# Linear attention and MLP on one core: full-width matmuls for the ninth chunk, another schedule for batches 0 and 1

## The chip, the cores and the metric

The kernel runs on one core of one Trainium2 chip. The metric is device time in microseconds (us). Before the change it is 336.48 us, the median of three runs (336.4 to 340.16). The profile is one execution; its span is about 2 us shorter than the timed runs, so spans are compared with spans and times with times. Every run compared here is in the fast state; one timed run of one experiment was slow (322.38 us in e7, where the other three took 316.51 to 321.17), and it is left out of the ratio.

TensorE is called PE, its weight loads PEld, VectorE DVE, ScalarE ACT, and SP the engine whose queue issues most transfers. Names of tiles in the code and the profiles: `eq` is exp(q), `eqT` its transpose, `ek` and `ekr` are exp(k) of the 512 rows and of the remainder, `vm` and `vr` the cast v of the two, `pkv` the PSUM tile of kv, `po` that of the attention's output, `xn` and `xnT` the normalised x and its transpose, `ptr` the PSUM tile of a transpose on PE.

## The reference, cut to what matters

```python
# q, k, v: 8 batches, 8 heads, 576 rows, 64 columns
q_s = softmax(q, over the 64 columns)
k_s = softmax(k, over the 576 rows)
kv  = einsum('bhsd,bhse->bhde', k_s, v)        # 64 x 64 for each head
x   = einsum('bhsd,bhde->bhse', q_s, kv)       # heads side by side: 576 x 512
xn  = (x - mean) / sqrt(var + 1e-6) * g_ln     # over the 512
out = x + relu(xn @ w_ch1) @ w_ch2             # 512 -> 2048 -> 512
```

A batch has 576 rows: 512 of them make one chunk of four blocks of 128 rows, and 64 remain. The kernel gathers the eight remainders into a ninth chunk, two batches to a block of 128 rows.

## The kernel before

Chunk c's MLP is a list of PE steps, and the work that prepares later chunks is hung between them at step numbers. Each engine is given its instructions in this order; in the traces below ACT (8.93 us) and DVE (2.96 us) stand still at one that waits for a transfer, with work that is ready behind it. `mm1` is the first layer (`ph`, then relu into `hT`), `mm2` the second (`pc`, then `ot`). In chunk 0 there are 128 steps of `mm1` with 256 columns and 64 steps of `mm2`; in the others 64 and 64, all of 512 columns (only the last block of chunk 8's `mm2` is cut into 32 of 256).

```python
    def po_mm(c, t, i):
        if i == 0:
            pobox["p"] = att_ps.tile([P, DM], FP32, tag="a", name="po")   # 2 PSUM buffers
        po = pobox["p"]
        j = i % NP
        if c < B:
            nc.tensor.matmul(po[:, j*P : j*P+P], eqTs[c][:, t, j, :], kv_sb[:, c, j, :],
                             start=True, stop=True)
        else:                        # ninth chunk: one batch = 64 of the 128 rows
            ps = slice(64 * (i // NP), 64 * (i // NP) + 64)
            nc.tensor.matmul(po[ps, j*P : j*P+P], eqTs[c][:, t, j, ps],
                             kv_sb[:, 2*t + i // NP, j, :], start=True, stop=True)

    def x_out(c, t):                 # divide by the softmax sum, then the statistics
        x = xs[c][0]
        nc.vector.tensor_mul(x[:, t]..., pobox["p"]..., eqs[c][2][:, t].to_broadcast([P, H, D]))
        stats(c, t, x[:, t])         # bn_stats, bn_aggr, xn: all on DVE

    def prep_side(b, a0, a1):        # exp_q, one DMA transpose of exp(q), exp_k, casts, sums
        ...
    def load_batch(b):               # allocate; three DVE memsets; k, v, q, then the remainders
        ...
    # first_batch() ...
        for i in (2, 0, 1):          # q, k, v of batch 1 wait for a part of w1
            nc.gpsimd.tensor_copy(out=raws[1][i][0:1, 0, 0, 0:1], in_=w1_sb[0:1, 0, 1024:1025])
            load_main(nc.sync, 1, i, 0, H)
        load_kvrem(nc.sync, 1)
        nc.gpsimd.tensor_copy(out=gate, in_=raws[1][2][:, 0, 0, 0:4])
        for g4 in range(4):
            load_w2(g4)
        ...
        for t in range(T):
            sum_q(0, t)
            nc.vector.tensor_mul(eq[:, t], eq[:, t], rq[:, t].to_broadcast([P, H, D]))
            eq_pT(0, t, nc.vector)   # PE transpose, copied out of PSUM by DVE
    # ... [cut]
        run(mlp_steps(0), [(90, lambda: load_batch(2))]
            + prep_side(1, 20, 70) + attn_side(1, 56, 76, 78, 108, True))
        for c in range(1, B):
            if c == 1:
                side += prep_side(2, 4, 50); side += attn_side(2, 40, 60, 64, 96)
            elif c + 1 < B:
                side += attn_side(c + 1, 2, 22, 26, 58)
            else:
                side += attn_side(C9, 0, 0, 20, 60)
            if c + 2 < B:
                side += [(1, lambda b=c + 2: load_batch(b))]
                side += prep_side(c + 2, 90 if c == 1 else 66, 126)
```

The softmax here doesn't subtract the row's maximum and nothing guards it: scores larger than these inputs give would overflow.

## Time and profile before

Stages are cut at the first `mm1` matmul of each chunk, read from the timeline or the chain of waits (which differ by up to 0.2 us).

| stage | us | PE busy | granted clock |
|---|---|---|---|
| first attention, to 29.7 | 29.7 | 8.93 | 0.90 |
| chunk 0 (with batch 1's attention) | 51.5 | 38.94 | 0.83 |
| chunk 1 | 35.2 | 31.01 | 0.95 |
| chunks 2 to 6, each | 29.8 | 29.70 | 1.00 |
| chunk 7 (with the ninth chunk's attention) | 36.6 | 36.49 | 1.00 |
| chunk 8 and the tail | 31.9 | 27.59 | 1.00 |

A full chunk costs 29.8 us, so the excess lies in the beginning and in chunk 7. The view of busy time by stretch of the kernel before says the same; its columns are stretch, length, busy us (and count) of each engine, granted PE clock, share of the DMA engines (it can read above 1: 1.03 in a stretch further down) and GB/s:

```profile
29.70:81.20 51.50, 38.94 (x246) 25.18 (x247) 22.77 (x49) 13.16 (x26) 4.30 (x7) 0.83 0.78 162
81.20:116.40 35.20, 31.01 (x164) 14.77 (x164) 21.77 (x51) 17.57 (x34) 2.20 (x4) 0.95 0.75 182
116.40:146.20 29.80, 29.70 (x163) 14.47 (x164) 22.05 (x51) 13.54 (x25) 2.98 (x5) 1.00 0.80 195
265.40:302.00 36.60, 36.49 (x160) 15.14 (x160) 13.48 (x22) 8.86 (x16) 2.16 (x4) 1.00 0.15 44
```

The waits of PE in the kernel before, longest first (engine, line and tile that waited, what it waited for: us in total, times, longest):

```profile
PE ptr L452 <- DVE eq L512: 15.3, 4, 9.0
PE ptr L452 <- DVE xn L268: 7.4, 7, 2.2
PE po L253 <- DMA eqT<-eq: 7.1, 2, 3.5
PE pkv L221 <- ACT ek L133: 4.2, 1, 4.2
PE pkv L221 <- DVE vr L148: 1.1, 1, 1.1
```

PE waited twice, 3.5 us each, for a DMA transpose of exp(q): once in chunk 0 and once in chunk 1 (15.86 and 7.65 us of transpose in the chain of waits). In chunk 7 PE is never idle, and still it takes 6.8 us too long. Where the time goes shows in the weight loads of the timeline there (start, length, engine, line, operation, shape; in brackets the idle time before it):

```profile
270.36 0.11 PEld L259 LDWEIGHTS <-eqT 128*64 128x64 bf16 x1 [0.42 <-issue]
270.53 0.10 PEld L306 LDWEIGHTS <-w_sb 128*128 128x128 bf16 x1
270.85 0.11 PEld L259 LDWEIGHTS <-eqT 128*64 128x64 bf16 x1 [0.23 <-issue]
271.03 0.10 PEld L306 LDWEIGHTS <-w_sb 128*128 128x128 bf16 x1
271.35 0.11 PEld L259 LDWEIGHTS <-eqT 128*64 128x64 bf16 x1 [0.23 <-issue]
```

A load of 64 columns sits behind an idle gap of 0.23 or 0.42 us, and from one half matmul to the next, with one 512-column matmul between them, 0.49 us pass. The 512-column matmul alone needs 0.216 (8.63 us for 40 of them in the chain of waits), so the half one costs 0.28 us. Why a half-width load has this gap no run here shows; e1 below shows that the cost goes with the half width: chunk 7 falls from 36.6 to 31.7 us.

### The profile page before, as it was taken

Reading aid. Unit: us, or ns where it says so; the run is one execution under the profiler, and the core shown is the slowest. Engines: PE = TensorE matmul, PEld = TensorE weight load, DVE = VectorE, ACT = ScalarE, POOL = GpSimd, SP = SyncE. Lnnn points to the kernel's source line nnn. Section 1 sums busy time; section 2 is a strip of 40 time slices with the busy share of each in tenths; the row PEclk is TensorE's granted clock in tenths of the full one; section 3 lists DMA queues with packets and bytes.
Section 4 is the critical chain, followed back from the end, with each engine's and each line's share of the span. In section 5 each row is a group of like instructions: output and inputs, shape, how many; then the busy total and the mean of one; then the engine's idle time right before and its main releaser. Section 6 shows DMA issues by size and latency. Waiting matters only on the chain.

```text
span 333.9 us, 4180 instructions
## 1 busy us (share of the span) xinstructions
PE 291.4 (87%) x1603; PEld 148.3 (44%) x1620; DVE 180.5 (54%) x389; ACT 123.7 (37%) x227; POOL 32.4 (10%) x62
## 2 busy tenths in 40 slices
PE   0257575799959999999999999999999999999994
PEld 0154454444424454455445544544554433444443
DVE  4754267705426959745962874597279215520112
ACT  4315432301962055625804551581353043205500
POOL 4403000002000110110010011002000100010021
PEclk9995969699998999999999999999999999999999
DMA  9999994922990859939996962958106201111023
GB/s 204 204 192 329 229 143 59 347 50 92 299 207 2 188 168 309 175 82 359 177 207 204 266 135 80 331 128 159 63 2 119 101 33 31 31 63 65 0 47 79
DMA packets 76643, 49.74 MB, mean 149 GB/s; under 512 B 45392, under 2 KB 74320, under 8 KB 76624
## 3 DMA queue, kind: packets, MB, share of 16 engines
q1 hardware_dynamic: 67872, 35.26, 44.6%
q0 software_dynamic: 8752, 14.22, 17.8%
q8 instruction: 12, 0.20, 0.3%
q14 instruction: 7, 0.06, 0.1%
HBM read 36.96 MB, written 9.44 MB: 139 GB/s over the span
## 4 chain that ended last, share of the span: by engine, by line
PE 73%; DMA 15%; DVE 7%; SPq 1%; issue 1%; POOL 1%
PE ph L306 33%; PE pc L353 29%; DMA eqT<-eq 7%; PE pc L364 4%; DMA w_sb<-in_moe_w_ch_dram 3%; DMA ktr<-in_k_dram 3%; DMA kt<-in_k_dram 2%; PE pkv L221 2%; DVE st L266 2%; PE po L259 2%; PE po L253 2%; DVE x L276 2%; SPq L105 1%; DVE xn L268 1%; PE pc L375 1%
## 5 line engine op out<-in xcount | busy, mean ns | idle before, releaser
L306 PE MATMUL ph<-xnT,w_sb 128*128 128x512 bf16 x512 | 128.6, 380 | 0.4 <-DVE rq L178 0.4
L294 ACT ACTIVATE hT<-ph 128x512 bf16<-128x512 f32 x112 | 66.9, 597 | 134.8 <-PE ph L306 134.8
L353 PE MATMUL pc<-w_sb,hT 128*128 128x512 bf16 x481 | 110.0, 382 | 1.0 <-issue 0.2
L353 PEld LDWEIGHTS <-hT 128*128 128x128 bf16 x496 | 47.7, 98 | 58.0 <-DVE hT L292 2.3
L306 PEld LDWEIGHTS <-w_sb 128*128 128x128 bf16 x512 | 45.6, 98 | 48.2 <-DMA xnT<-xn 0.9
L335 DVE SCALAR_TENSOR_TENSOR ot<-pc,rstd,x 128x512 f32<-128x512 f32 (+1 forms) x37 | 27.1, 732 | 52.1 <-PE pc L353 36.3
L341 POOL DMA_DIRECT2D out_dram<-ot x32 | 18.1, 565 | 251.9 <-DVE ot L335 240.3
L253 PE MATMUL po<-kv_sb,eqT 128*128 128x128 bf16 x128 | 26.8, 227 | 7.7 <-DMA eqT<-eq 7.1
L276 DVE TENSOR_TENSOR x<-po,rq 128x512 bf16<-128x512 f32 x32 | 22.0, 687 | 19.0 <-PE po L259 13.0
L221 PE MATMUL pkv<-vm,ek 128*128 128x129 bf16 x112 | 25.5, 229 | 4.2 <-ACT ek L133 4.2
L177 DVE TENSOR_REDUCE zq<-eq 128x8 f32<-128x512 bf16 x36 | 23.7, 659 | 5.5 <-ACT eq L165 5.5
L268 DVE SCALAR_TENSOR_TENSOR xn<-x,mv,g_bc 128x512 bf16<-128x512 bf16 x32 | 24.1, 752 | 1.1
L292 DVE TENSOR_SCALAR hT<-ph 128x512 bf16<-128x512 f32 x16 | 11.0, 688 | 22.4 <-PE ph L306 22.4
L320 PE MATMUL ph<-xnT,w_sb 128*128 128x256 bf16 x128 | 22.9, 328 | 0.0
L266 DVE BATCH_NORM_STATS2 st<-x 128x6 f32<-128x512 bf16 x32 | 22.2, 694 | 1.1
L253 PEld LDWEIGHTS <-eqT 128*128 128x128 bf16 x128 | 12.6, 102 | 20.5 <-DMA eqT<-eq 7.8
L165 ACT ACTIVATE eq<-qt 128x512 bf16<-128x512 f32 x32 | 18.0, 621 | 6.4 <-DMA qt<-in_q_dram 6.0
L133 ACT ACTIVATE ek<-kt 128x512 bf16<-128x512 f32 x32 | 18.2, 620 | 1.9 <-DMA kt<-in_k_dram 1.7
L320 PEld LDWEIGHTS <-w_sb 128*128 128x128 bf16 x128 | 14.3, 118 | 4.8 <-issue 1.3
L221 PEld LDWEIGHTS <-ek 128*128 128x128 bf16 x128 | 13.4, 108 | 5.5 <-ACT ek L133 4.5
L452 PE MATMUL ptr<-ident,eq 128*128 128x128 bf16 x16 | 2.4, 306 | 15.3 <-DVE eq L512 15.3
L364 PE MATMUL pc<-w_sb,hT 128*128 128x512 bf16 x62 | 14.7, 393 | 0.3 <-issue 0.2
(66 smaller groups left out, 147.7 us busy)
## 6 DMA issues: line engine op xcount, KB each, us to landing
out_dram<-ot POOLq DMA_DIRECT2D x32, 256.0 KB, 3.2
qt<-in_q_dram SPq DMA_DIRECT2D x7, 1024.0 KB, 12.9
kt<-in_k_dram SPq DMA_DIRECT2D x7, 1024.0 KB, 7.4
vt<-in_v_dram SPq DMA_DIRECT2D x7, 1024.0 KB, 9.6
w_sb<-in_moe_w_ch_dram POOLq DMA_DIRECT2D x8, 512.0 KB, 11.3
qt<-in_q_dram SPq DMA_DIRECT2D x2, 512.0 KB, 4.3
ktr<-in_k_dram SPq DMA_DIRECT2D x8, 128.0 KB, 11.3
kt<-in_k_dram SPq DMA_DIRECT2D x4, 256.0 KB, 8.2
```

The lines of the kernel that those rows point to most:

```text
L177: nc.vector.reduce_sum(zq[:, t], eq[:, t], axis=AX.X)
L221: nc.tensor.matmul(pkv[:, j % 2, 0:w], lhsT, rhs, start=(t == 0), stop=(t == T))
L253: nc.tensor.matmul(po[:, j * P : j * P + P], eqTs[c][:, t, j, :], kv_sb[:, c, j, :], start=True, stop=True,)
L266: nc.vector.bn_stats(st[:, t], src)
L268: nc.vector.scalar_tensor_tensor(xn[:, t], in0=src, scalar=mv[:, t, 0:1], in1=g_bc, op0=ALU.subtract, op1=ALU.mult,)
L276: nc.vector.tensor_mul(x[:, t].rearrange("p (h d) -> p h d", h=H), pobox["p"].rearrange("p (h d) -> p h d", h=H), eqs[c][2][:, t].to_broad ...
L294: nc.scalar.activation(dst, src, AF.Relu)
L306: nc.tensor.matmul(hbox["ph"], w1_sb[:, ko, m * P : (m + 1) * P], xnTs[c][:, :, ko, :], start=(ko == 0), stop=(ko == KO1 - 1),)
L320: nc.tensor.matmul(hbox["ph"][:, m % 2], w1_sb[:, ko, m * P : (m + 1) * P], xnTs[c][:, ts, ko, :], start=(ko == 0), stop=(ko == KO1 - 1),)
L335: nc.vector.scalar_tensor_tensor(ot, in0=pc, scalar=rstds[c][:, t : t + 1], in1=xs[c][0][:, t, cols], op0=ALU.mult, op1=ALU.add,)
L353: nc.tensor.matmul(hbox["pc"], hbox["h"][:, ko, t, :], w2_sb[:, ko, :], start=(ko == 0), stop=(ko == KO2 - 1),)
L364: nc.tensor.matmul(hbox["pc", t], hbox["h"][:, ko, t, :], w2_sb[:, ko, :], start=(ko == 0), stop=(ko == KO2 - 1),)
```

## The change

The intent has three parts. The ninth chunk's output matmul takes two batches at once: 128 rows of exp(q) against the kv of both batches, 256 columns, of which each half of the rows uses its own 128. Batch 1 is handled as batch 0 already was: exp(q) is divided by its sum before the transpose, so statistics read PSUM directly and ACT copies x. For both, the statistics now come ahead of that copy, and batch 0's transposed copies move from DVE to ACT. Batch 1's transpose moves from DMA to PE, and its attention moves behind `mm1` of chunk 0, whose halves get another order. The loads of batch 1 and of w2 are gated one by one, and batches 2 and 3 are loaded later. (A load is gated by a tiny copy into its destination that reads a piece of the weights: it can't be issued before that piece has landed. In the changed kernel the copy for batch 1's q waited 6.33 us for the transfer of w1 and ran at 21.89 us, and the load was issued at 22.09.) The diff, cut to its core:

```diff
     def po_mm(c, t, i):
+            # ninth chunk; one PSUM tile for each two i
+            if i % 2 == 0:
+                pobox[i // 2] = att_ps.tile([P, 2, 2, P], FP32, tag="a", name="po")
             nc.tensor.matmul(
-                po[ps, j * P : j * P + P], eqTs[c][:, t, j, ps],
-                kv_sb[:, 2 * t + i // NP, j, :], start=True, stop=True,
-            )
+                pobox[i // 2][:, i % 2], eqTs[c][:, t, i, :],
+                kv_sb[:, 2 * t : 2 * t + 2, i, :], start=True, stop=True,
+            )
+            if i % 2 == 1:          # two multiplies of 64 x 256: each half takes its own columns
+                for half in range(2):
+                    nc.vector.tensor_mul(x[ps, hs, :]..., pobox[i // 2][ps, :, half]..., ...)
     def x_out(c, t):
+        if c < 2:
+            stats(c, t, pobox["p"])
+            nc.scalar.copy(x[:, t], pobox["p"])
+            return
     def mlp_steps(c):               # chunk 0
-                for n in range(4) for h in range(2)
+            order = [(0, 0), (1, 0), (0, 1), (1, 1), (2, 0), (2, 1), (3, 0), (3, 1)]
     def first_batch():
+        gated(2, w1_sb[0:1, 0, 512:513])     # q of batch 1 after the second part of w1
         load_kvrem(nc.sync, 1)
+        gated(0, w1_sb[0:1, 0, 1024:1025])   # k after the third
+        load_w2(0)
+        gated(1, w1_sb[0:1, 0, 1536:1537])   # v after the fourth
+        nc.gpsimd.tensor_copy(out=gate, in_=raws[1][0][:, 0, 0, 0:4])
+        for g4 in range(1, 4): load_w2(g4)
         ...
+        for t in range(T):
+            norm_q(0, t)                      # sum, reciprocal, multiply: DVE
+        for j in range(NP):
+            eq_pT(0, j, nc.scalar)            # copies now on ACT
+            exp_k(0, j)
     # chunk 0
-            [(90, lambda: load_batch(2))]
-            + prep_side(1, 20, 70)
-            + attn_side(1, 56, 76, 78, 108, True),
+            spread([lambda j=j: exp_q(1, j) for j in range(NP)], 60, 84)
+            + [(98, lambda: prep_kvrem(1))]
+            + spread([lambda t=t: norm_q(1, t) for t in range(T)], 84, 120)
+            + spread([lambda t=t: eq_pT(1, t, nc.vector) for t in range(T)], 108, 128)
+            + spread([lambda j=j: exp_k(1, j) for j in range(NP)], 112, 136)
+            + spread([lambda j=j: cast_v(1, j) for j in range(NP)], 130, 144)
+            + attn_side(1, 142, 150, 150.5, 165, [160, 168, 176, 184])
+            + [(176, lambda: load_batch(2))],
     # chunk 1
-                side += prep_side(2, 4, 50)
-                side += attn_side(2, 40, 60, 64, 96)
+                side += prep_side(2, 12, 50)
+                side += attn_side(2, 50, 66, 68, 94)
-                side += [(1, lambda b=c + 2: load_batch(b))]
+                side += [(40 if c == 1 else 1, lambda b=c + 2: load_batch(b))]
```

More of the change, by code (lines that the diff above doesn't have):

```diff
@@ L246, in po_mm @@
     def po_mm(c, t, i):
-        if i == 0:
-            pobox["p"] = att_ps.tile([P, DM], FP32, tag="a", name="po")
-        po = pobox["p"]
-        j = i % NP
         if c < B:
+            if i == 0:
+                pobox["p"] = att_ps.tile([P, DM], FP32, tag="a", name="po")
             nc.tensor.matmul(
-                po[:, j * P : j * P + P], eqTs[c][:, t, j, :], kv_sb[:, c, j, :],
+                pobox["p"][:, i * P : i * P + P], eqTs[c][:, t, i, :], kv_sb[:, c, i, :],
                 start=True, stop=True,
@@ L257, in po_mm @@
         else:
-            ps = slice(64 * (i // NP), 64 * (i // NP) + 64)
+            if i % 2 == 0:
+                pobox[i // 2] = att_ps.tile([P, 2, 2, P], FP32, tag="a", name="po")
             nc.tensor.matmul(
-                po[ps, j * P : j * P + P], eqTs[c][:, t, j, ps],
-                kv_sb[:, 2 * t + i // NP, j, :], start=True, stop=True,
-            )
+                pobox[i // 2][:, i % 2], eqTs[c][:, t, i, :],
+                kv_sb[:, 2 * t : 2 * t + 2, i, :], start=True, stop=True,
+            )
+            if i % 2 == 1:
+                hs = slice(2 * i - 2, 2 * i + 2)
+                x = xs[c][0][:, t].rearrange("p (h d) -> p h d", h=H)
+                for half in range(2):
+                    ps = slice(64 * half, 64 * half + 64)
+                    nc.vector.tensor_mul(
+                        x[ps, hs, :].rearrange("p (j h) d -> p j h d", h=2),
+                        pobox[i // 2][ps, :, half].rearrange("p j (h d) -> p j h d", h=2),
+                        eqs[c][2][ps, t, hs].rearrange("p (j h) -> p j h", h=2).to_broadcast([64, 2, 2, D]),
+                    )
     def stats(c, t, src):
@@ L275, in x_out @@
         x = xs[c][0]
-        nc.vector.tensor_mul(
-            x[:, t].rearrange("p (h d) -> p h d", h=H),
-            pobox["p"].rearrange("p (h d) -> p h d", h=H),
-            eqs[c][2][:, t].to_broadcast([P, H, D]),
-        )
+        if c < 2:
+            stats(c, t, pobox["p"])
+            nc.scalar.copy(x[:, t], pobox["p"])
+            return
+        if c < B:
+            nc.vector.tensor_mul(
+                x[:, t].rearrange("p (h d) -> p h d", h=H),
+                pobox["p"].rearrange("p (h d) -> p h d", h=H),
+                eqs[c][2][:, t].to_broadcast([P, H, D]),
+            )
         stats(c, t, x[:, t])
@@ L383, in mlp_steps @@
         if c == 0:
+            order = [(0, 0), (1, 0), (0, 1), (1, 1), (2, 0), (2, 1), (3, 0), (3, 1)]
             return [
                 (lambda m=m, h=h, ko=ko: mm1_half(c, m, h, ko))
-                for n in range(4) for h in range(2)
+                for n, h in order
                 for m in range(4 * n, 4 * n + 4) for ko in range(KO1)
@@ L424, in prep_side, with attn_side @@
         return s
-    def attn_side(c, kv0, kv1, po0, po1, pe=False):
+    def attn_side(c, kv0, kv1, po0, po1, pe=None):
         s = []
@@ L433, in attn_side @@
             )
-        n = NP if c < B else 2 * NP
         fns = []
         for t in range(T):
-            fns += [lambda t=t, i=i: po_mm(c, t, i) for i in range(n - 1)]
-            fns.append(lambda t=t: (po_mm(c, t, n - 1), x_out(c, t)))
+            fns += [lambda t=t, i=i: po_mm(c, t, i) for i in range(NP - 1)]
+            fns.append(lambda t=t: (po_mm(c, t, NP - 1), x_out(c, t)))
         s += [(po0, lambda: start_x(c))] + spread(fns, po0, po1)
         if pe:
-            w = (po1 - po0) / T
-            s += [(po0 + w * (t + 1) + 12, lambda t=t: xn_pT(c, t, nc.scalar)) for t in range(T)]
+            s += [(pe[t], lambda t=t: xn_pT(c, t, nc.scalar)) for t in range(T)]
         else:
@@ L445, in attn_side, with norm_q @@
             s.append((po1 + 12, lambda: xn_T(c, 2, 2)))
-        s.append((127, lambda: rstd_op(c)))
+        s.append((pe[-1] + 0.5 if pe else 127, lambda: rstd_op(c)))
         return s
+    def norm_q(b, t):
+        eq, zq, rq = eqs[b]
+        sum_q(b, t)
+        nc.vector.tensor_mul(eq[:, t], eq[:, t], rq[:, t].to_broadcast([P, H, D]))
     def pe_T(dst, src, t, eng):
@@ L490, in first_batch, with gated @@
         nc.gpsimd.tensor_copy(out=gate, in_=raws[0][0][:, 3, 0, 0:4])
+        alloc_batch(1)
+        def gated(which, src):
+            nc.gpsimd.tensor_copy(out=raws[1][which][0:1, 0, 0, 0:1], in_=src)
+            load_main(nc.sync, 1, which, 0, H)
         for nb in range(4):
@@ L496, in first_batch @@
                 )
-        alloc_batch(1)
-        for i in (2, 0, 1):
-            nc.gpsimd.tensor_copy(out=raws[1][i][0:1, 0, 0, 0:1], in_=w1_sb[0:1, 0, 1024:1025])
-            load_main(nc.sync, 1, i, 0, H)
+        gated(2, w1_sb[0:1, 0, 512:513])
         load_kvrem(nc.sync, 1)
-        nc.gpsimd.tensor_copy(out=gate, in_=raws[1][2][:, 0, 0, 0:4])
-        for g4 in range(4):
+        gated(0, w1_sb[0:1, 0, 1024:1025])
+        load_w2(0)
+        gated(1, w1_sb[0:1, 0, 1536:1537])
+        nc.gpsimd.tensor_copy(out=gate, in_=raws[1][0][:, 0, 0, 0:4])
+        for g4 in range(1, 4):
             load_w2(g4)
-        eq = None
         for j in range(NP):
             exp_q(0, j)
-        eq, zq, rq = eqs[0]
+        nc.scalar.activation(ekr[0:SR, 0], raws[0][3][0:SR], AF.Exp)
         for t in range(T):
-            sum_q(0, t)
-            nc.vector.tensor_mul(
-                eq[:, t], eq[:, t], rq[:, t].to_broadcast([P, H, D])
-            )
-            eq_pT(0, t, nc.vector)
-        nc.scalar.activation(ekr[0:SR, 0], raws[0][3][0:SR], AF.Exp)
+            norm_q(0, t)
         for j in range(NP):
+            eq_pT(0, j, nc.scalar)
             exp_k(0, j)
+        for j in range(NP):
             for t in range(T + 1):
@@ L525, in first_batch @@
                     po_mm(0, t, i)
-                nc.scalar.copy(xs[0][0][:, t], pobox["p"])
-                stats(0, t, pobox["p"])
+                x_out(0, t)
             if t >= 1:
```

## The prediction

> **What bounds it now.** The page: PE is busy 87% of a 333.9 us span; the chain of waits is 73% PE, 15% DMA. By the busy-by-stretch view: first attention 0–29.7 us; chunk 0's MLP (carrying batch 1's attention) 29.7–81.2, 51.5 us with PE busy 38.9 at a mean clock of 0.83; chunk 1 81.2–116.4, 35.2 us; chunks 2 to 6 29.8 us each with PE full; chunk 7 (carrying the ninth chunk's attention) 36.6 us, also full; chunk 8 and the tail 31.9. So 29.8 is a chunk's floor; the excess is 21.7 us in chunk 0, 5.4 in chunk 1, 6.8 in chunk 7.
>
> **What the change does.**
>
> 1. *Chunk 7.* 32 matmuls of half the array become 16 full ones of 256 columns. In the timeline 4 half matmuls and 5 of 512 columns take 2.20 us, of which the 5 need 1.08; so a half matmul costs 0.28 us (32 cost 9.0 us), against 0.058 for a full one of 128 columns elsewhere. 256 columns start 0.109 us apart at full clock in chunk 0 [...]. 16 × 0.11 = 1.8 us: **−7.2 us**, chunk 7 at 29.4. DVE gets 16 multiplies of 64x256, about 0.42 us each (estimate between 0.30 for 128 columns and 0.69 for 512), +4 us; it was busy 13.5 of 36.6, so at most a small stall.
>
> 2. *First batch.* The transposed copies leave DVE for ACT, so the rounds of sum, reciprocal, multiply, 2.68 us apart now, come about 1.65 apart; kv starts near 14.4 instead of 17.35. Statistics before the x copy removes a DVE wait of about 0.6. MLP 0 starts near 25.9: **−3.8 us**.
>
> 3. *Chunk 0.* PE waits now: 4.2 for ek (late k), 1.1 for vr, 3.5 for eqT (a DMA transpose of 15.9 us among weight loads), then up to 2 us at a time for xn behind DVE; and idling halves the clock ([...]here 256-column matmuls at 0.213 instead of 0.109). The transpose goes to PE (16 × 0.06), k's remainder is loaded earlier, the attention moves behind mm1. I add 0.109 × 108 + 4.3 cold, 2.0 transposes, 13.8 for mm2, 2.1 attention, and stalls of about 6 us (eq_pT waiting for norm_q on DVE, 3–4; po for its two PSUM buffers, about 2). Chunk 0 lasts about 40 us and ends near 66: **−15 in all** with step 2.
>
> 4. *Chunk 1.* Batch 2's load is issued near 61.5, its q lands near 73, and ACT's first exp_q blocks the relus for some 5 us; six PSUM buffers hide most. Batch 3's load stands behind eqT(2) in the DMA queue; its eqT(3) stands before the second half of xnT(2), which I expect near 101.5 while mm2 ends near 97.5: about 4 us of PE waiting on DMA xnT. Chunk 1 stays near 35 us.
>
> Sum: 15 + 0 + 7 = 22 us; chunks 2 to 6 unchanged.
>
> **Prediction: 314 us, range 307 to 321. Faster by over 2%: 0.97; within 2%: 0.02; slower: 0.01.**
>
> **Signs.** Right if MLP 0's first matmul is at 25–27 us; chunk 0 ends at 62–69; chunk 2 starts at 98–105, after a PE wait on xnT; chunk 7 is 29–31 without 0.4 us gaps in weight loads; no eqT DMA before 70 us.
>
> **What would make it wrong.** w2 or v landing late (mm2 waits for DMA near 48–55 us); q of batch 2 landing after 76 (chunk 1 stalls more); or queue order harmless (chunk 2 at 96: 308). If DVE's 16 small multiplies cost more, chunk 7 loses 1–3 us.

## The result, and the profile after

The changed kernel takes 319.15 us, the median of four runs (318.17 to 321.89), against 337.18 for the kernel before in the same rounds. The ratio is 0.9463, with a 95% interval of 0.9379 to 0.9547. Ratios here are the mean time of one kernel's fast runs over the mean of the other's fast runs of the same rounds, so they are not quite the ratio of the medians.

| stage | before | expected | after |
|---|---|---|---|
| first attention | 29.7 | 25.9 | 25.6 |
| chunk 0 | 51.5 | 40 | 38.9 |
| chunk 1 | 35.2 | 35 | **39.0** |
| chunks 2 to 6, each | 29.8 | 29.8 | 29.8 |
| chunk 7 | 36.6 | 29.4 | **31.7** |
| chunk 8 and the tail | 31.9 | 31.9 | 32.0 |

The stretches of the changed kernel:

```profile
25.60:64.50 38.90, 34.19 (x262) 23.17 (x261) 24.56 (x53) 16.00 (x32) 3.82 (x7) 1.00 0.73 168
64.50:103.50 39.00, 32.89 (x165) 15.18 (x164) 21.44 (x50) 17.38 (x34) 2.16 (x4) 0.91 0.86 232
103.50:133.30 29.80, 29.80 (x164) 14.46 (x164) 22.51 (x53) 13.54 (x25) 2.98 (x5) 1.00 0.79 197
252.66:284.38 31.72, 29.85 (x146) 13.85 (x144) 17.56 (x34) 8.87 (x16) 2.16 (x4) 1.00 0.18 51
```

and the waits of PE in it:

```profile
PE ptr L472 <- DVE eq L467: 14.9, 7, 9.0
PE ph L321 <- ACT hT L309: 5.5, 1, 5.5
PE ptr L472 <- DVE xn L278: 3.1, 4, 1.4
PE po L259 <- DVE x L268: 1.9, 2, 1.1
PE po L252 <- ACT x L288: 1.4, 1, 1.4
PE ph L321 <- DMA xnT<-xn: 0.5, 1, 0.5
```

The waits for the DMA transpose of exp(q), for ek and for vr are gone. The two largest new ones are 5.5 us of `mm1` for ACT in chunk 1, and 1.9 us of the ninth chunk's po for DVE. The first is put down to ACT's relu, but the timeline of ACT shows what ACT itself waited for:

```profile
67.31 0.60 ACT L309 ACTIVATE hT<-ph 128x512 bf16<-128x512 f32 x1 [0.27 <-PE ph L321]
76.83 0.63 ACT L165 ACTIVATE eq<-qt 128x512 bf16<-128x512 f32 x1 [8.93 <-DMA qt<-in_q_dram]
77.37 0.58 ACT L309 ACTIVATE hT<-ph 128x512 bf16<-128x512 f32 x1
```

Between two relus stands the first exp of batch 2's q. Its transfer was issued at 61.30 us and landed 15.5 us later. ACT takes its work in order, so the relus behind it waited as well: the next one ran at 77.37, after that exp, though the matmuls it reads from had ended by 72.5. PE ran on until its six PSUM buffers were full, at 72.5 us, and then waited. Its clock was lowered by that wait, as the stretches after it and PE's timeline show:

```profile
64.00:76.00 12.00, 8.46 (x40) 3.72 (x38) 2.80 (x6) 1.81 (x4) 1.46 (x3) 1.00 1.03 308
76.00:84.00 8.00, 6.00 (x16) 2.15 (x16) 3.81 (x12) 7.17 (x15) 0.00 (x0) 0.57 0.37 67
```

```profile
64.52 7.93 PE L321 MATMUL ph<-xnT,w_sb 128*128 128x512 bf16 x36
78.00 5.91 PE L321 MATMUL ph<-xnT,w_sb 128*128 128x512 bf16 x14 [5.54 <-ACT hT L309]
```

The 14 matmuls after the wait took 5.91 us; at 0.216 each they are 3.0. So the wait cost 5.5 us and the low clock after it about 2.9 more: 8.4 of the 9.2 us by which this chunk exceeds 29.8. In this trace the matmuls of 512 columns were 0.427 us apart after the 5.5 us wait, and 0.216 again only from 83.8 us, 5.8 us after the work resumed.

In chunk 7 the weight loads of the changed kernel have no gap any more:

```profile
257.36 0.10 PEld L259 LDWEIGHTS <-eqT 128*128 128x128 bf16 x1
257.58 0.21 PEld L321 LDWEIGHTS <-w_sb 128*128 128x128 bf16 x2
257.90 0.10 PEld L259 LDWEIGHTS <-eqT 128*128 128x128 bf16 x1
258.12 0.42 PEld L321 LDWEIGHTS <-w_sb 128*128 128x128 bf16 x3
```

DVE in the same stage:

```profile
262.40 1.74 DVE L268 TENSOR_TENSOR x<-po,rq 64x256 bf16<-64x256 f32 x4
264.17 0.69 DVE L276 BATCH_NORM_STATS2 st<-x 128x6 f32<-128x512 bf16 x1
264.90 0.18 DVE L277 BATCH_NORM_AGGREGATE mv<-st 128x2 f32<-128x6 f32 x1
265.11 0.75 DVE L278 SCALAR_TENSOR_TENSOR xn<-x,mv,g_bc 128x512 bf16<-128x512 bf16 x1
265.90 1.75 DVE L268 TENSOR_TENSOR x<-po,rq 64x256 bf16<-64x256 f32 x4
```

From one block's multiplies to the next 3.50 us pass without a gap, while PE offers a block each 10 steps, 2.6 us with its share of po. That is where the 1.9 us of waiting come from.

### The profile page after: what moved, and what is told of

Read it like the earlier page. It is cut to its first block, busy times and chain, and to the rows that moved or that the text cites. A ratio compares the mean times of both kernels' runs of the same rounds, so it can differ in the third digit from the quotient of the medians.

```text
span 316.4 us, 4221 instructions
## 1 busy us (share of the span) xinstructions
PE 283.5 (90%) x1620; PEld 145.9 (46%) x1620; DVE 184.8 (58%) x401; ACT 127.7 (40%) x235; POOL 32.8 (10%) x62
## 4 chain that ended last, share of the span: by engine, by line
PE 75%; DVE 13%; DMA 7%; ACT 1%; issue 1%; SPq 0%; ACTq 0%
PE ph L321 32%; PE pc L368 30%; DMA qt<-in_q_dram 6%; PE pkv L221 3%; PE ph L335 3%; PE pc L379 3%; DVE st L276 3%; DVE xn L278 2%; PE po L252 2%; DVE eq L467 2%; DVE zq L177 2%; PE pc L390 1%; DVE x L268 1%; DMA xnT<-xn 1%; ACT eq L165 1%
## 5 line engine op out<-in xcount | busy, mean ns | idle before, releaser
L368 PE MATMUL pc<-w_sb,hT 128*128 128x512 bf16 x496 | 110.3, 379 | 0.0
L321 PEld LDWEIGHTS <-w_sb 128*128 128x128 bf16 x512 | 47.1, 99 | 56.4 <-issue 9.9
L221 PE MATMUL pkv<-vm,ek 128*128 128x129 bf16 x112 | 23.7, 220 | 0.0
L278 DVE SCALAR_TENSOR_TENSOR xn<-x,mv,g_bc 128x512 bf16<-128x512 bf16 x28 | 21.1, 752 | 1.0
L276 DVE BATCH_NORM_STATS2 st<-x 128x6 f32<-128x512 bf16 x28 | 19.4, 695 | 1.0
L472 PE MATMUL ptr<-ident,eq 128*128 128x128 bf16 x32 | 4.0, 263 | 14.9 <-DVE eq L467 14.9
L291 DVE TENSOR_TENSOR x<-po,rq 128x512 bf16<-128x512 f32 x24 | 16.4, 685 | 1.1 <-PE po L252 0.9
L379 PE MATMUL pc<-w_sb,hT 128*128 128x512 bf16 x64 | 16.9, 379 | 0.0
L335 PE MATMUL ph<-xnT,w_sb 128*128 128x256 bf16 x128 | 16.4, 291 | 0.0
L227 DVE RECIPROCAL rzk<-pkv 128x2 f32<-128x2 f32 x14 | 2.4, 172 | 21.9 <-PE pkv L221 21.9
L139 DVE CAST vm<-vt 128x512 bf16<-128x512 f32 x28 | 10.8, 421 | 7.2 <-DMA vt<-in_v_dram 7.1
## 6 DMA issues: line engine op xcount, KB each, us to landing
ktr<-in_k_dram SPq DMA_DIRECT2D x8, 128.0 KB, 10.7
```

The source lines that it names most:

```text
L221: nc.tensor.matmul(pkv[:, j % 2, 0:w], lhsT, rhs, start=(t == 0), stop=(t == T))
L276: nc.vector.bn_stats(st[:, t], src)
L278: nc.vector.scalar_tensor_tensor(xn[:, t], in0=src, scalar=mv[:, t, 0:1], in1=g_bc, op0=ALU.subtract, op1=ALU.mult,)
L321: nc.tensor.matmul(hbox["ph"], w1_sb[:, ko, m * P : (m + 1) * P], xnTs[c][:, :, ko, :], start=(ko == 0), stop=(ko == KO1 - 1),)
L335: nc.tensor.matmul(hbox["ph"][:, m % 2], w1_sb[:, ko, m * P : (m + 1) * P], xnTs[c][:, ts, ko, :], start=(ko == 0), stop=(ko == KO1 - 1),)
L368: nc.tensor.matmul(hbox["pc"], hbox["h"][:, ko, t, :], w2_sb[:, ko, :], start=(ko == 0), stop=(ko == KO2 - 1),)
```

## The experiments

Eleven kernels ran. All gave correct results. The changed kernel itself was not run again in these calls, so a comparison of times with its 319.15 us goes from one call to another; the stages of the profiles are the firmer evidence. In e1 (faster by less than 2%) and e11 (its interval reaches across 2%) the interval still lies below 1. Chunk starts and ends come from the timeline of each one's profile.

| run | edit | median us | ratio to before | 95% interval |
|---|---|---|---|---|
| the change | | 319.15 | 0.9463 | 0.9379–0.9547 |
| e1_ninth_only | before + the ninth chunk's part | 331.43 | 0.9850 | 0.9812–0.9889 |
| e2_load_early | change, batch 2 loaded at step 132 | 311.05 | 0.9243 | 0.9215–0.9271 |
| e3_q_first | change, q first in that load | 319.46 | 0.9483 | 0.9444–0.9522 |
| e4_ninth_spread | change, po over steps 8–60 | 317.24 | 0.9426 | 0.9382–0.9470 |
| e5_batch1_as_before | change, batch 1 in the old way | 321.01 | 0.9548 | 0.9500–0.9595 |
| e6_old_gates | change, loads gated in the old way | 324.52 | 0.9675 | 0.9611–0.9739 |
| e7_dma_transpose | change, DMA transpose for batch 1 | 320.33 | 0.9492 | 0.9412–0.9572 |
| e8_copy_first | change, ACT copy ahead of the statistics | 319.81 | 0.9535 | 0.9473–0.9597 |
| e9_load_and_spread | change, step 132, po over 6–62 | 308.90 | 0.9197 | 0.9150–0.9245 |
| e10_norm_earlier | e9 + batch 1's exp_q, norm_q earlier | 306.64 | 0.9120 | 0.9096–0.9145 |
| e11_load3_at_40 | before + batch 3 loaded at step 40 | 330.94 | 0.9824 | 0.9778–0.9870 |

### e1: the ninth chunk alone

```diff
 # the kernel before, with po_mm and x_out of the ninth chunk from the change; 4 po steps a block
-        n = NP if c < B else 2 * NP
+        n = NP
```

> The kernel before with the ninth chunk's part alone. Theory (a half-array matmul costs 0.28 us, a full one of 256 columns 0.11 us, less 1.9 us that PE loses waiting for DVE to free the two PSUM buffers): chunk 7 falls from 36.6 to about 31.7 us and the whole by about 4.9 us, to about 332 us (ratio 0.985); nothing before chunk 7 moves by more than 0.5 us. Rival (the ninth chunk gained only because the earlier change shifted the loads or the clock): chunk 7 stays at 36 us or more, ratio 0.995 or above.

Measured: 331.43 us, ratio 0.9850. Chunk 7 goes from 265.64 to 297.36 us, which is 31.7, and PE waits for DVE there 1.9 us, as in the changed kernel. The theory holds, and the rival falls: this part is worth about 5 us by itself, independent of the rest.

### e2: batch 2 loaded earlier

```diff
-            + [(176, lambda: load_batch(2))],
+            + [(132, lambda: load_batch(2))],
```

> The changed kernel with the load of batch 2 issued at step 132 of chunk 0 (about 47 us) in place of step 176 (60 us). Theory: chunk 1's 39.0 us hold a wait for q of batch 2, 5.5 us on PE, and about 3 us of half clock after it; the DMA engines are idle from 51 to 60 us, so the load fits there, q lands before 64 us, chunk 1 falls to 30 to 31.5 us with full clock, the whole to 309 to 312 us. Rival A (q is late because the DMA engines lack the bandwidth): the load collides with the last weights, chunk 0 gets longer or q lands as late, gain under 2 us. Rival B (the second half of xn's DMA transpose would have held chunk 2 anyway, behind eqT of batch 3 in the queue): q is early, but chunk 2 starts no earlier than 101 us, gain about 2 us.

Measured: 311.05 us. The loads are issued from 48.75 us on, ACT never waits for q, and chunk 1 runs from 66.34 to 96.91 at full clock:

```profile
66.30:96.90 30.60, 30.02 (x165) 14.54 (x164) 21.34 (x50) 17.48 (x34) 2.16 (x4) 1.00 0.78 208
```

Moving one load by 44 steps gained 8 us. Both rivals fall: the DMA engines had room (their share read 0.00 from 52 to 60 us in the changed kernel), and the transpose of xn did not hold chunk 2. Chunk 0 ended at 66.3 here, not 64.5; in three other kernels with the same chunk 0 or nearly so (e3, e4, e9) it ended at 65.5 to 65.7, so about 1 us of this is the run, in part when PE's clock rises (the first 108 matmuls took 13.6 us in the changed kernel and 13.9 to 14.7 in these four), and 0.7 us more is a wait for the load of g_ln in this run's first attention.

### e3: q first in the queue

```diff
-        for which in range(3):
+        for which in ((2, 0, 1) if b == 2 else range(3)):
```

> The changed kernel with q of batch 2 loaded ahead of k and v, at the same step. Theory (ACT takes its work in order, so the relus stand behind whichever exp waits for a transfer): q lands near 70 us instead of 76.8, the four exp_q run then, but the exp of k's remainder, whose load comes last, now holds ACT until about 76; PE gets to m = 12 before its six PSUM buffers are full, so its wait shrinks from 5.5 to about 1 us and the half clock after it goes: gain 4 to 7 us, 312 to 315 us. Rival (the amount of data, not the order, sets the wait): gain under 2 us.

Measured: 319.46 us, no gain; here the rival named the size rightly. The exps of q no longer waited, and ACT then stood at the remainder of k for 5.55 us, as the theory said. But PE's waits were not lost, only renamed:

```profile
PE pkv L221 <- ACT ek L133: 3.2, 1, 3.2
PE ph L321 <- DMA xnT<-xn: 3.1, 1, 3.1
```

Chunk 2 started at 103.4 us, as in the changed kernel (103.5). Batch 3's loads were issued at 82.2 us against 82.9, and the transposes of batch 3's exp(q) and of xn stand behind them in the same queue. So in the changed kernel two waits lie close behind one another: that for q of batch 2, and the one for xn's second transpose that the prediction had named. The first hides the second. That second wait had its price here: `mm1` ran at half clock after it (matmuls of 512 columns 0.43 us apart until 105.9 us, 0.22 from 106.3), and chunk 2 took 31.2 us in place of 29.8. Only an earlier load removes both (e2, e9 and e10 wait 0 to 0.5 us for xnT).

### e4: the ninth chunk's matmuls further apart

```diff
-                side += attn_side(C9, 0, 0, 20, 60)
+                side += attn_side(C9, 0, 0, 8, 60)
```

> The changed kernel with the ninth chunk's po matmuls spread over steps 8 to 60 of chunk 7 instead of 20 to 60. Theory (chunk 7's 31.7 us are 29.8 us of PE work and 1.9 us of waiting for DVE, which needs 3.5 us for each of the four blocks while PE offers one each 2.6 us): one block each 3.3 us, the wait falls to under 0.4 us, chunk 7 to 29.5 to 30.2 us, the whole by about 1.8 us, to 317.3 us. Rival (the wait comes from the relu and statistics that stand in DVE's order, whatever the spacing): the wait stays over 1.2 us.

Measured: 317.24 us. PE's wait for DVE fell from 1.9 to 0.5 us, and chunk 7 to 30.1 us (253.88 to 283.97):

```profile
PE po L259 <- DVE x L268: 0.5, 1, 0.5
```

The times of the two kernels overlap, so the gain of 1.6 us is shown by the stage, not by the whole. With steps 6 to 62, in e9, the wait is gone from the list and chunk 7 takes 29.65 us.

### e5: batch 1 handled as before

```diff
-        if c < 2:      # x_out
+        if c < 1:
-            spread([lambda j=j: exp_q(1, j) for j in range(NP)], 60, 84) + ...   # the new chunk 0
+            [(90, lambda: load_batch(2))] + prep_side(1, 20, 70)
+            + attn_side(1, 56, 76, 78, 108, [97.5, 105, 112.5, 120]),
```

> The changed kernel with batch 1 handled in chunk 0 as before the change (sums without division, one DMA transpose of exp(q), attention among mm1, batch 2 loaded at step 90); first batch, gates and ninth chunk stay changed. Theory (chunk 0's gain comes from moving the attention behind mm1 and from the PE transposes, and part of it was given back in chunk 1 by loading batch 2 late): po waits for the DMA transpose until 45 to 50 us, chunk 0 ends at 74 to 78 us in place of 64.5, but chunk 1 has no wait for q and takes 30 to 34 us, so chunk 2 starts at 106 to 111 us in place of 103.5 and the whole is 322 to 327 us. Rival (the gates and the first batch alone made chunk 0 shorter): chunk 0 ends before 68 us.

Measured: 321.01 us, a little under the range. Chunk 0 ended at 75.25 us (10.7 later than with the change), and chunk 1 took 30.5 us (8.5 less), so chunk 2 started at 105.8 in place of 103.5. The sums fit, but the reason given for chunk 0 was wrong. The DMA transpose of exp(q) did not hold po. It was kv that waited, for the cast of v:

```profile
PE pkv L221 <- DVE vm L139: 8.3, 1, 8.3
PE ptr L472 <- DVE xn L278: 6.8, 7, 1.6
PE po L252 <- DVE kv_sb L230: 1.8, 2, 1.5
```

The cast started at 40.92, when v landed. So the new place of the attention, behind `mm1`, is good because k and v land near 38 and 41 us under the new gates; and as shipped the net worth of batch 1's new handling as a whole (place, transposes, division) is only 2.3 us, because the late load of batch 2 gives most of it back. With that load moved (e2), chunk 2 starts at 96.9, 8.9 us before e5. In the old place the new gates gain little: e5's chunk 0 takes 49.7 us, 51.5 before the change.

### e6: the old order of the gates

```diff
-        gated(2, w1_sb[0:1, 0, 512:513]); load_kvrem(nc.sync, 1)
-        gated(0, w1_sb[0:1, 0, 1024:1025]); load_w2(0)
-        gated(1, w1_sb[0:1, 0, 1536:1537]); gate on k; load_w2(1..3)
+        for i in (2, 0, 1): gated(i, w1_sb[0:1, 0, 1024:1025])
+        load_kvrem(nc.sync, 1); gate on q; load_w2(0..3)
```

> The changed kernel with the loads gated as before the change (q, k, v of batch 1 all when the third quarter of the first weights has landed, then the remainders; second weights when q has landed). Theory (the remainder of v stands at the end of the queue and lands near 42 us or later, the cast of it stands in DVE's order before norm_q of t = 2): PE's wait for norm_q grows by 2 to 4 us near 43 us, chunk 0 ends at 66.5 to 69, chunk 1 loses as much or a little less, the whole is 320 to 323 us. Rival (the order of the gates does not matter once the attention is behind mm1): chunk 0 ends within 1 us of 64.5 to 65.6.

Measured: 324.52 us, more than expected. The mechanism is the expected one: the cast of v's remainder waits for its transfer in front of the third norm_q,

```profile
44.57 0.42 DVE L148 CAST vr<-vtr 64x512 bf16<-64x512 f32 x1 [2.96 <-DMA vtr<-in_v_dram]
```

and PE's wait before the third transpose grew from 1.85 to 4.71 us:

```profile
46.71 0.61 PE L472 MATMUL ptr<-ident,eq 128*128 128x128 bf16 x4 [4.71 <-DVE eq L467]
```

The size was off. After this wait the clock had dropped (matmuls of 256 columns 0.213 us apart, and the first 14 of `mm2` took 3.76 us against 3.19). Chunk 0 ended at 69.5, 5 us later than with the change, but 0.9 us of that is the run: the first 108 matmuls, before the wait, took 14.5 us in place of 13.6. From the 109th on chunk 0 lasted 29.4 us, against 25.2 to 26.0 in the six kernels with the new schedule and gates (the change, e2, e3, e4, e8, e9). The new gates are worth about 4 us in the new schedule.

### e7: a DMA transpose in place of the PE transposes

```diff
-            + spread([lambda t=t: eq_pT(1, t, nc.vector) for t in range(T)], 108, 128)
+            + [(120.5, lambda: eq_T(1))]
```

> The changed kernel with batch 1's four PE transposes of exp(q) and their DVE copies replaced by one DMA transpose after norm_q, all else left. Theory (the DMA transpose is slow among the weight loads): PE's 3 us of waits for norm_q near 40 to 46 us go, but po waits for the transpose until 52 to 58 us where it started at 51.8; net chunk 0 ends 0 to 4 us later, 65 to 69 us. Rival (the schedule alone made the gain, the PE transposes cost more than they save): chunk 0 ends 1 to 3 us earlier, 62 to 63.5 us.

Measured: 320.33 us, the median of all four runs; ratio 0.9492 against 0.9463. `mm2` started at 41.25 us in place of 45.66, since PE no longer waited for norm_q, but then kv waited 1.8 us for the cast of v and po 3.2 us for the transpose. Chunk 0 ended at 66.0 us. Against kernels with the same chunk 0 (64.5 to 65.7) that is 0.3 to 1.5 us. Counted from the 109th matmul of `mm1`, which leaves the rise of the clock out, chunk 0 lasted 27.0 us, against 25.2 to 26.0 in the six kernels named under e6. So the PE transposes are not where most of the gain comes from; they seem worth 1 to 1.8 us, from one profile of this run.

### e8: the copy of x ahead of the statistics

```diff
-            stats(c, t, pobox["p"])
-            nc.scalar.copy(x[:, t], pobox["p"])
+            nc.scalar.copy(x[:, t], pobox["p"])
+            stats(c, t, pobox["p"])
```

> The changed kernel with the ACT copy of x before the statistics for batches 0 and 1, as before the change. Theory (two engines that read the same PSUM tile are taken in program order, so the first block's statistics wait for a copy of 0.55 us): mm1 of chunk 0 starts 0.5 to 0.7 us later, at 26.1 to 26.3 us, po of batch 1 likewise, the whole within 1.5 us of the changed kernel. Rival (the order does not matter): the first block's statistics start at the same time after po, 0.3 us or less.

Measured: 319.81 us. The first statistics start at 19.23 us in place of 18.57, behind a wait for ACT, and a later block waits 0.20 us more:

```profile
19.23 0.70 DVE L276 BATCH_NORM_STATS2 st<-po 128x6 f32<-128x512 f32 x1 [1.08 <-ACT x L287]
22.73 0.70 DVE L276 BATCH_NORM_STATS2 st<-po 128x6 f32<-128x512 f32 x1 [0.20 <-ACT x L287]
```

`mm1` of chunk 0 starts at 26.5 us in place of 25.55, 0.9 and not 0.5 to 0.7 us later. In the whole this is inside the noise of the times (the profiled run was the slowest of the four, 322.99 us, and PE also waited 2.8 us before its chunk 2). The statistics and the copy both only read the tile `po`, and the trace shows them one after the other: ACT's copy from 18.61 us, the statistics from 19.23.

### e9 and e10: the two repairs together, and one more

```diff
 # e9
-            + [(176, lambda: load_batch(2))],
+            + [(132, lambda: load_batch(2))],
-                side += attn_side(C9, 0, 0, 20, 60)
+                side += attn_side(C9, 0, 0, 6, 62)
 # e10: also
-            spread([... exp_q(1, j) ...], 60, 84) ... norm_q 84, 120 ... eq_pT 108, 128
+            spread([... exp_q(1, j) ...], 44, 60) ... norm_q 64, 104 ... eq_pT 94, 126
```

> The changed kernel with batch 2's load at step 132 and the ninth chunk's po matmuls over steps 6 to 62. Theory (the two gains are in different stages, 8.1 and 1.5 to 1.9 us): they add, 309 to 310 us, chunk 7 at 29.8 to 30.2 us. Rival (one eats the other): not below 310.7 us.

> As e9_load_and_spread, with batch 1's exp_q at steps 44 to 60, norm_q at 64 to 104 and the PE transposes at 94 to 126 of chunk 0. Theory (q of batch 1 lands near 30 us and DVE needs 6.5 us for norm_q, so PE's 3 us of waits before the transposes come from norm_q starting at 37 us): these waits fall under 1 us, chunk 0 ends 2 to 3 us earlier, 306.5 to 308 us. Rival (DVE is the limit of the stretch in any order, or q comes too late): gain under 1 us.

Measured: 308.90 and 306.64 us. In e9 the two gains add (311.05 less 2.15, just under the expected 309 to 310). In e10 PE's waits before batch 1's transposes fall to 0.59 us for norm_q and 0.62 us for a buffer, from 3.1 us in the changed kernel, and chunk 0 ends at 63.2 us, 2.3 earlier than e9's 65.56. e10 is the fastest kernel here: 29.7 us, or 8.8%, under the kernel before. Its stretches:

```profile
25.60:63.20 37.60, 34.75 (x262) 23.63 (x261) 24.45 (x53) 15.90 (x32) 3.79 (x7) 1.00 0.97 243
63.20:93.80 30.60, 30.02 (x166) 14.55 (x165) 21.32 (x50) 17.37 (x34) 2.16 (x4) 1.00 0.78 208
243.15:272.80 29.65, 29.55 (x145) 14.03 (x144) 17.55 (x34) 8.86 (x16) 2.16 (x4) 1.00 0.19 54
```

Chunks 1 and 7 now stand within 1 us of the 29.8 us of a full chunk.

### e11: one line of the change on the kernel before

```diff
-                side += [(1, lambda b=c + 2: load_batch(b))]
+                side += [(40 if c == 1 else 1, lambda b=c + 2: load_batch(b))]
```

> The kernel before with one line of the change: batch 3 loaded at step 40 of chunk 1 in place of step 1. Theory (in chunk 1 of before, the DMA transpose of batch 2's exp(q) stood in the queue behind five loads of batch 3 and po waited 3.5 us for it, with half clock after): eqT is issued near 87 us in place of 92, po does not wait, chunk 1 falls from 35.2 to 30 to 31.5 us, the whole by 4 to 5 us, to about 332 us (ratio 0.986 to 0.988). Rival (the later load of batch 3 holds the second half of xn's transpose as long): ratio 0.995 or above.

Measured: 330.94 us, ratio 0.9824 (0.9778 to 0.9870). The DMA transpose of batch 2's exp(q) is issued at 85.87 us, with nothing before it:

```profile
85.87 1.95 SPq L181 DMA_TRANSPOSE eqT<-eq  x1
```

In the kernel before the queue ran:

```profile
83.26 2.63 SPq L105 DMA_DIRECT2D qt<-in_q_dram  x1
85.95 4.30 SPq L113 DMA_DIRECT2D ktr<-in_k_dram  x1
90.30 1.57 SPq L113 DMA_DIRECT2D vtr<-in_v_dram  x1
91.98 5.51 SPq L181 DMA_TRANSPOSE eqT<-eq  x1
```

With the line changed, chunk 1 takes 30.3 us (80.65 to 110.92). So this one line is worth about 5 us, and the prediction did not see it: it named the new place of that load only as a cost.

## Why the prediction was right, and where its sizes were off

The time (314 us, 307 to 321) held: the measured 319.15 lies inside the range. The predicted change was 22 us and the measured one 18.

- *What bounded the kernel*: right. Nothing changed in chunks 2 to 6 and 8.
- *The first batch*, predicted −3.8 us with `mm1` at 25.9: measured 25.55, −4.2. In the traces kv starts at 14.0 in place of 17.5, after rounds of sum, reciprocal and multiply 1.6 us apart in place of 2.7, so most of it lies there, where the transposed copies left DVE; no run isolates that. e8 shows 0.9 us of it to be the order of statistics and copy, where 0.6 was predicted.
- *Chunk 0*, predicted to end near 66 with about 6 us of stalls: it ended at 64.5. Its waits are 0.27, 1.85 and 0.95 us for norm_q and 1.4 for the PSUM buffers. e10 confirms the norm_q term by removing most of it. The PE transposes, to which the prediction gave credit, are worth 1 to 1.8 us by e7's profile; what counts more is that the attention no longer comes before its data (e5) and that the gates bring the remainders earlier (e6). No run isolates the new order of `mm1`'s halves, or the division before the transpose.
- *Chunk 1*, predicted at about 35 us, measured at 39.0: this is the mis-sized term, the landing of q and the wait behind it. The prediction put the landing of q at 73 us, held that "six PSUM buffers hide most" of ACT's wait, and put about 4 us on xn's transpose. q landed at 76.8, ACT waited 8.9 us, PE 5.5, and the half clock cost 2.9 more; the wait for xnT measured 0.5. That the miss is only 4 us is partly luck: the 4 us put down for xnT stood in for part of these 8.4. The prediction had named the late q ("landing after 76") among what would make it wrong, but not in its sum. The low clock after a wait had been counted for the beginning of chunk 0, but not here. e2 shows that all of this hung on the step of one load, and e3 that the wait for xnT was there, behind the other.
- *Chunk 7*, predicted −7.2 us, measured −4.9. The PE part was right: 31.7 us less the 1.9 us wait is 29.8, and e9 reached 29.65 once DVE kept up. The multiply was sized rightly, at 0.42 us; a block now has four of them, 1.74 us, where one of 128x512 took 0.69. The failed step is "at most a small stall": DVE's share of the whole stage was compared, where the 10 us in which po is offered decide. There a block takes 3.5 us of DVE and 2.6 us of PE.
- *Transposes in the queue*: right in kind, but the gain in e11 was not named, since the prediction did not ask why chunk 1 took 35.2 us before (its sum for chunk 1 leaves that wait out without saying why it goes). Of the two waits of 3.5 us for the DMA transpose in the list of waits, it treated only the one in chunk 0.
- *The signs*: `mm1` of chunk 0 at 25.55 us, the end of chunk 0 at 64.5 and no DMA transpose of exp(q) before 80.5 held. Chunk 2 started at 103.5, inside the 98 to 105, but after 0.5 us of waiting for xnT, so for another reason than the one given. Chunk 7 at 31.7 us missed its 29 to 31.

The parts can't simply be added. The ninth chunk gives 4.9 us and the first batch 4.2, each in a stage of its own. The rest acts on the same stretch, and what it is worth depends on the other parts: the new gates about 4 us (in the new schedule), the later load of batch 3 5 us (in the old one), the new handling of batch 1 2.3 us as shipped and 8.9 us with batch 2's load moved.

## What to carry to other kernels

When work is moved later, move the loads of what follows by what the DMA engines have free, not along with it: here they idled from 52 to 60 us (share 0.00) while the next load waited for its step number. Ask of every in-order engine what stands behind an instruction that waits for a transfer, and reckon with the slow clock after a PE wait of several microseconds: 5.5 us brought it here, and 4.2 us, with 1.1 us more soon after, in the kernel before (256 columns 0.213 us apart from 42.4 to 47.7 us). At 3.5 us it is not certain: of the two such waits in the kernel before, the one that ended at 52.79 left the matmuls at full spacing (0.109 us for 256 columns), the one that ended at 99.68 slowed them (0.427 for 512 columns) until 102.4. Compare an engine's demand with its supply over the few microseconds in which they meet, since the share of the stage says little.

## A half-width matmul between full ones, and the reading of the clock

- In the kernel before, a weight load of 64 columns came 0.23 or 0.42 us after the load before it had ended and the pair cost 0.28 us, against 0.056 for most full ones of 128 columns (`po` of the other chunks); 32 of them cost 9.0 us.
- In the changed kernel the view of stretches reads a granted clock of 1.00 from 25.6 to 64.5 us, though the first 108 matmuls of 256 columns took 13.61 us (0.126 each, against the 0.109 of most later ones in the stage), the first 16 of them 0.213 us apart. Spacing of matmuls is the safer reading.
